# Two-kind attention and a max-out layer: casts by single heads, half copies, identity matmuls in TensorE's early gaps, and SyncE's closing block at another place in the code

## The chip, the cores and the metric

One core of one Trainium2 chip. The metric is the time of one execution on the device, in microseconds (us). A core has five engines with queues of their own: TensorE (PE; its weight loads are shown as PEld), VectorE (DVE), ScalarE (ACT), GpSimd (POOL) and SyncE (SP), which here issues every DMA.

## The reference

Attention over 4 batches of 8 heads, 768 tokens, 64 numbers a head, and on its output a layer that takes the larger of two products:

```
scores = q @ k.T / sqrt(64)
keep   = causal                                  for "retrieval" heads (3 of the 8: 0, 2, 6)
keep   = causal & (key < 4 | query - key < 64)   for the others
a      = softmax(where(keep, scores, -1e9))
x      = concat over heads of (a @ v)            [3072, 512]
out    = maximum(x @ w1, x @ w2) @ w_out         w1, w2: [512, 1024], w_out: [1024, 512]
```

All inputs and the output are float32. `is_retrieval` is data, so which heads are of which kind is known only when the program runs.

## The kernel before

**Two programs in one.** The kernel sorts the heads at run time. If exactly three are retrieval heads, a branch (`tc.If`, L830) takes the program `run(..., exact=True)`; otherwise it takes a general one. Each engine has both in its code, one behind the other, and behind them a closing block (the rows of L870) that all engines run at the end. With these inputs the first branch is taken, so at its end every engine jumps over the second.

**The order is planned.** `run` doesn't issue instructions. It records operations in a plan: a function that emits them, a cost for each engine that could do it, what it depends on, its buffers and a priority. `Plan.schedule` then plays time forward with these costs, gives each operation to the engine that can start it first, and the operations are emitted in the order of their planned starts. So a cost that is changed changes which engine does what, and in which order, all through the kernel. Each engine runs its own list strictly in that order.

**Attention.** Work goes by pairs of heads, four pairs a batch, 16 in all (`pair`). For a pair SyncE loads q, k and v, one DMA for each head (L671); into nine `ld` buffers, so three pairs' loads can be under way. Each DMA waits for the one eight before it. In batch 0 the first half of all of v comes ahead of everything (L320). Casts to bf16 (L300 on DVE and POOL, L298 on ACT) make `qb` and `vb`; six transposes each on TensorE (L692) turn q and k, and a copy of 768 columns brings them from PSUM to `qk` (`tok` sets the tokens in order). Scores (L578) come in tiles of two banks, the mask is added by matmuls with the identity in batch 0 (L586) or multiplied in later; ACT takes the exponential (L599); TensorE multiplies by v (L623) into one of two `po` banks, and DVE normalises (L639, L642) into `xs`. In the exact program one `po` bank is given over to the general PSUM pool after the second half-unit (`PO_TWO`, L640 to L646).

**The layer.** max(x w1, x w2) w_out is rewritten as relu(x (w1 - w2)) w_out + x (w2 w_out). So the weights are prepared once: casts of w2 and w_out (`w_bf`, `wo_bf`), the difference `wd_bf` (L443), transposes of w2 (L452, copied into the tile `raw`) and the product of w2 and w_out (L463, into `wm_bf`). They are loaded in quarters of 512 KB, on the same SyncE queue as q, k and v; `EARLY` names the one that is issued first, and `LATER` gives the others a priority in units of pairs. For each batch `x_turn` transposes x, and `dense` does the products (L756, L780, L787), the relu (L764, L766) and the store (L793).

**The start.** A block of 42 identity matmuls (L418) is the first operation on TensorE, planned at `WARM` = 4.6 us:

```
def warm(e, bk=bk):
    for _ in range(int(WARM / 0.107)):
        nc.tensor.matmul(bk.t[:, 0, 0:128], lhsT=ident, rhs=ident, start=True, stop=True)
```

Of the kernel before, what the change touches and what calls it, by code (L numbers as in the profile page):

```python
# [10 lines left out]
BF16 = mybir.dt.bfloat16  # L11
I32 = mybir.dt.int32
ALU = mybir.AluOpType
ACT = mybir.ActivationFunctionType
# [156 lines left out]
DMA_FIRST = -2.2  # L171
# [1 line left out]
WIDE_PAIRS = (1, 1, 1, 1, 1, 1, 1, 1, 1, 0, 0, 0, 0, 0, 0, 0)  # L173
X_XBAR = (0, 1, 1, 1)
EARLY = (('wo', 3),)
LATER = {('w2', 0): 3.93, ('w2', 1): 3.55, ('w2', 2): 3.4, ('w2', 3): 3.03, ('w1', 0): 5.86, ('w1', 1): 4.21, ('w1', 2): 6.83, ('w1', 3): 6.11, ('wo', 0): 3.53, ('wo', 1): 1.32, ('wo', 2): 0.84, ('wo', 3): 0.93}
MASK_TO = 1
NORM = 0.80
PO_TWO = 2
DUO_FROM = 1  # L180
WARM = 4.6

SHIFT = {}
HOLD = {}
# [3 lines left out]
def kernel(  # L188
# [19 lines left out]
    nc = tc.nc  # L208
    V = nc.vector
    B, H, S, D = q.shape  # L210
# [28 lines left out]
    ident = tl("ident", [128, 128])  # L239
# [51 lines left out]
    po_t = psum("po", 2)  # L291
# [4 lines left out]
    def copy(e, o, i):  # L296
        if e == "ACT":
            nc.scalar.copy(out=o, in_=i)  # L298
        else:
            issued[e].append((V if e == "DVE" else nc.gpsimd).tensor_copy(out=o, in_=i).ins)  # L300
# [75 lines left out]
    def run(full, head, col, exact):  # L376
        P = Plan(*((SHIFT, HOLD) if exact else ({}, {})))
# [4 lines left out]
        sc_p, po_p, mm_p = map(Pool, map(list, (sc_t, po_t, mm_t) if PO_TWO or not exact else (sc_t, po_t[:1], po_t[1:] + mm_t)))  # L382
# [27 lines left out]
                            in1=causal, op0=ALU.mult, op1=ALU.add)  # L410
            c_m = P.op(f, {"DVE": 5.0}, [d_ir], prio=-20)

        if exact:
            bk = Buf(mm_p)

            def warm(e, bk=bk):
                for _ in range(int(WARM / 0.107)):
                    nc.tensor.matmul(bk.t[:, 0, 0:128], lhsT=ident, rhs=ident, start=True, stop=True)  # L418
            P.op(warm, {"PE": WARM}, (), [bk], prio=-100)
        d_w = {}  # L420
        for name in ("w2", "w1", "wo"):
            for c in range(4):
                if (name, c) in EARLY:
                    P.number += 1
                else:
                    d_w[name, c] = P.op(lambda e, name=name, c=c: load_weight(name, c), {"SP": 0.5},
                                        prio=LATER[name, c], size=0.524, rate=0.35)

        def landed(*keys):

            return dict(deps=[d_w[k] for k in keys if k in d_w],
                        ready=max([0.0] + [DMA_FIRST + 6.05 + 1.7 * EARLY.index(k) for k in keys if k in EARLY]))
        wd_ops, w2_ops, wo_ops, wm_ops, w2t_ops = [], [], [], [], []
        for c in range(4):
            w2_ops.append(P.op(lambda e, c=c: copy(e, w2_bf[(slice(None),) + quarter(c)], w_raw[1][(slice(None),) + quarter(c)]),
# [10 lines left out]
        for fch in range(FC):  # L446
            bk = Buf(mm_p)
# [6 lines left out]
            o = P.op(tr, {"PE": 0.23}, w2_ops[2 * (fch // 4):2 * (fch // 4) + 2], [bk], prio=300 + fch)  # L454
# [15 lines left out]
        last_exp, last_score, last, last_open, units = [None], [None], [None], [None], [0]  # L470
# [50 lines left out]
        def attend(b, p, qk, vb, tk, ov, r):  # L521
# [110 lines left out]
            for u in range(2):  # L632
                rz = Buf(rz_p)

                def norm(e, u=u, rz=rz):
                    nh = 2 if exact else 1
                    p4 = po[u].t[:, 0, 0:nh * nn * (D + 1)].rearrange("p (h n e) -> p h n e", h=nh, e=D + 1)
                    rz_ = rz.t.rearrange("p (h n) -> p h n", h=nh)
                    V.reciprocal(out=rz_, in_=p4[:, :, :, D])  # L639
                    for i in range(nh):  # L640
                        h, n0 = (i, u * nn) if exact else (u, 0)
                        V.tensor_tensor(out=xs[b].t[:, n0:n0 + nn, bass.ds(col(s0 + h), D)], in0=p4[:, i, :, 0:D],  # L642
                                        in1=rz_[:, i].unsqueeze(2).to_broadcast([128, nn, D]), op=ALU.mult)
                done.append(P.op(norm, {"DVE": NORM}, [o for o in prev[u] if o], [po[u], rz, xs[b]], prio=r))
                for g in [u] if exact else range(NG):
                    norms[b][g].append(done[-1])  # L646
                units[0] += 1
                if exact and units[0] == PO_TWO:
                    spare = Buf(po_p)
                    spare.users = 1  # L650
                    P.op(lambda e: None, {"SP": 0.0}, [done[-1]], [spare], prio=-50).then = lambda: (
                        mm_p.free.append((spare.free, len(mm_p.tiles))), mm_p.tiles.append(spare.t))
            return done[-1]

        def tok(t):
            return t.rearrange("c (p n) -> c p n", n=NB)

        def pair(b, p):
            r = b * HP + p
            s0 = 2 * p  # L660
            if p == 0:
                xs[b], xt[b], xt_ops[b], norms[b] = Buf(xs_p), Buf(xt_p), [], ([], [])
            raws, loads = [], []
            for i, src in enumerate((q, k, v)):
                t = Buf(ld)
                raws.append(t)
                order, rate = ("(p n)", WIDE) if wide[r] and src is not v else ("(n p)", NARROW)
                two = []
                n0 = NB // 2 if b == 0 and src is v else 0
                for h in range(2):  # L670
                    two.append(P.op(lambda e, t=t, src=src, h=h, order=order, n0=n0: nc.sync.dma_start(  # L671
                        out=t.t[:, h, n0:], in_=src[b, bass.ds(head(s0 + h), 1), 128 * n0:].rearrange(
                            f"o {order} d -> p (o n) d", p=128)),
                        {"SP": 0.5}, (), [t], prio=r + 0.01 * i, size=0.0983 if n0 else 0.197, rate=rate))
                loads.append(two)
            qk, vb = Buf(qk_p), Buf(vb_p)
            tk, cast = [], []
            qb = Buf(qb_p)
            for i in range(2):
                def f(e, i=i):  # L680
                    for h in range(2):
                        copy(e, qb.t[:, i, :, h, :], raws[i].t[:, h])
                cast.append(P.op(f, {"POOL": 0.95, "DVE": 0.75} if b == 0 else {"POOL": 0.95}, loads[i],
                                 [raws[i], qb], prio=r + 0.01 * i, shared=True))
                if not wide[r]:
                    continue
                bk = Buf(mm_p)

                def tr(e, i=i, bk=bk):
                    psb = bk.t[:, 0].bitcast(BF16)  # L690
                    for n in range(NB):
                        nc.tensor.transpose(psb[:, n * 128:(n + 1) * 128],  # L692
                                            qb.t[:, i, n].rearrange("p h d -> p (h d)"), ident)
                o = P.op(tr, {"PE": 0.34}, [cast[i]], [qb, bk, qk], prio=90 + 2 * r)
                tk.append(P.op(lambda e, bk=bk, i=i: copy(
                    e, tok(qk.t[:, i]), bk.t[:, 0].bitcast(BF16)[:, 0:S].rearrange("c (n p) -> c p n", p=128)),
                               {"DVE": 0.90, "ACT": 0.7}, [o], [bk, qk], prio=r))
            if not wide[r]:
                tk.append(P.op(lambda e: nc.sync.dma_start_transpose(
                    out=qk.t.rearrange("c i (n p) -> c (i n) p", p=128),  # L700
                    in_=qb.t.rearrange("p i n h d -> p (i n h d)")),
                    {"SP": XBAR}, cast, [qb, qk], prio=r - 0.5, size=0.393, rate=0.2))
            n0 = NB // 2 if b == 0 else 0
# [13 lines left out]

            last[0] = attend(b, p, qk, vb, tk, ov, r)
# [91 lines left out]
                pool.free = []  # L810
        last[0].then = widen
        order = P.schedule()
        held = None
        with tc.manual_schedule():
            for o in order:
                for l in issued.values():
                    l.clear()
                o.emit(o.engine)
                if o.engine == "DVE" and o.shared:
                    held = issued["DVE"][-1]  # L820
                elif o.engine == "POOL" and held is not None:
                    tc.add_manual_dep(issued["POOL"][0], held.name, IN_TURN, reason="turns at the shared port")
                    held = None
# [51 lines left out]
```

## Time and profile before

| | |
|---|---|
| time, median of 6 runs | 189.69 us (189.13 to 191.44) |
| the profiled execution | 189.74 us, of which the span is 187.97 us |
| granted TensorE clock, mean over the span | 0.977 |
| busy: PE, PEld | 170.2 us (91%), 100.7 us (54%) |
| busy: ACT, DVE, POOL | 115.1 us (61%), 88.0 us (47%), 49.6 us (26%) |
| DMA | 36.96 MB, mean 197 GB/s |
| code: queue 8 (TensorE's) and 14 | 15 packets, 0.25 MB; 17 packets, 0.14 MB |

The page divides the span into 40 slices of 4.7 us. A digit is the busy share of a slice in tenths, and PEclk is the clock that was granted to TensorE, in tenths of full speed; where the trace records none, it stands at full. "SPq" and "PEldq" are rows of an engine's sequencer: waits, branches and DMA issues, in which the engine itself does nothing. A wait is put down to what came last before it ended. The chain that ended last is followed back from the last piece of work, and so says nothing of what comes behind it: the time from the last eviction to the end of the span is seen in the sequencers' rows alone.

### The profile page before, as it was taken

The numbers are of one execution on the slowest core, as the hardware profiler recorded it, in microseconds if no ns is written. First come the engines' busy times: TensorE is split into PE (matmuls) and PEld (weight loads), VectorE is DVE, ScalarE is ACT, GpSimd is POOL, SyncE is SP. The second block draws the span as 40 slices with busy tenths as digits, with TensorE's granted clock in tenths as the row PEclk, the third lists the DMA queues.
The fourth block names the chain that finished last, engine by engine and source line by source line (L and its number), as shares of the span: only waits on it lengthen the run. The fifth ranks groups of instructions, "written<-read, shape, count | busy, mean of one in ns | idle before, by whom it ended". The sixth has DMA issues, their size and how long they took to land.

```text
span 188.0 us, 4584 instructions
## 1 busy us (share of the span) xinstructions
PE 170.2 (91%) x1643; PEld 100.7 (54%) x1663; DVE 88.0 (47%) x247; ACT 115.1 (61%) x191; POOL 49.6 (26%) x107
## 2 busy tenths in 40 slices
PE   1859989699999999999999999999999999999950
PEld 1836756456756555654655555455545546445440
DVE  5647874868788385435575464446731000000000
ACT  3247898778888778727893395478836327337120
POOL 2101040556985864532026326010000000000000
PEclk9975999999999999999999999999999999999997
DMA  5999999999999999999999999991029221021040
GB/s 122 304 275 357 276 278 377 277 301 302 320 275 237 201 224 220 248 195 221 249 233 229 249 208 248 260 252 63 3 81 202 58 112 56 0 112 59 17 158 9
DMA packets 79554, 36.96 MB, mean 197 GB/s; under 512 B 68642, under 2 KB 73506, under 8 KB 79522
## 3 DMA queue, kind: packets, MB, share of 16 engines
q1 hardware_dynamic: 79522, 36.58, 77.2%
q8 instruction: 15, 0.25, 0.5%
q14 instruction: 17, 0.14, 0.2%
HBM read 25.17 MB, written 6.29 MB: 167 GB/s over the span
## 4 chain that ended last, share of the span: by engine, by line
PE 82%; DMA 4%; DVE 3%; ACT 2%; issue 2%; DVEq 0%; SPq 0%; POOL 0%; POOLq 0%
PE mm L756 12%; PE mm L780 11%; PE sc L578 9%; PE po L623 8%; PE po L756 8%; PE po L780 7%; PE mm L787 6%; PE sc L780 4%; PE po L787 3%; PE mm L463 3%; DMA raw<-in_moe_w_dram 3%; PE sc L756 2%; PE sc L787 2%; PE mm L692 2%; DMA ld<-in_k_dram 2%
## 5 line engine op out<-in xcount | busy, mean ns | idle before, releaser
L599 ACT ACTIVATE at_all<-sc 128x1024 bf16<-128x1024 f32 (+2 forms) x72 | 59.5, 870 | 6.6 <-PE sc L578 3.3
L756 PEld LDWEIGHTS <-wd_bf 128*128 128x128 bf16 x256 | 23.2, 98 | 14.0
L300 POOL CAST qb<-ld 128x384 bf16<-128x384 f32 x50 | 24.0, 507 | 18.9 <-DVE at_all L610 8.7
L756 PE MATMUL mm<-xt,wd_bf 128*128 128x384 bf16 x140 | 27.6, 326 | 0.0
L623 PE MATMUL po<-vb,at_all 128*128 128x65 bf16 x472 | 26.3, 195 | 0.8 <-POOL vb L300 0.7
L623 PEld LDWEIGHTS <-at_all 128*128 128x128 bf16 x472 | 21.6, 98 | 9.9 <-issue 2.1
L578 PE MATMUL sc<-qk 64*128 64x128 bf16 (+2 forms) x364 | 23.3, 242 | 1.9 <-ACT qk L298 0.9
L642 DVE TENSOR_TENSOR xs<-po,rz 128x192 f32 x64 | 22.9, 357 | 3.0 <-DVE rz L639 0.9
L780 PEld LDWEIGHTS <-raw 128*128 128x128 bf16 x152 | 14.1, 98 | 13.6
L578 PEld LDWEIGHTS <-qk 64*128 64x128 bf16 x364 | 12.7, 95 | 14.6 <-issue 9.4
L300 POOL CAST vb<-ld 128x384 bf16<-128x384 f32 (+1 forms) x28 | 12.9, 485 | 23.1 <-DVE qb L300 9.5
L639 DVE RECIPROCAL rz<-po 128x6 f32<-128x6 f32 x32 | 6.2, 194 | 26.4 <-PE po L623 26.3
L756 PE MATMUL po<-xt,wd_bf 128*128 128x384 bf16 x88 | 17.9, 326 | 0.0
L780 PE MATMUL mm<-wo_bf,raw 128*128 128x512 bf16 x59 | 15.5, 379 | 0.3
L610 DVE TENSOR_TENSOR at_all<-at_all,smk 128x1024 bf16<-128x1024 bf16 (+3 forms) x27 | 15.2, 583 | 0.0
L787 PEld LDWEIGHTS <-xt 128*128 128x128 bf16 x100 | 9.3, 97 | 9.3
L610 DVE TENSOR_TENSOR at_all<-at_all,tri 128x256 bf16<-128x256 bf16 (+1 forms) x36 | 9.7, 302 | 6.5 <-ACT at_all L599 6.4
L787 PE MATMUL mm<-wm_bf,xt 128*128 128x512 bf16 x48 | 12.3, 379 | 0.0
L298 ACT COPY ot<-mm 128x512 f32<-128x512 f32 x9 | 5.3, 586 | 11.1 <-PE mm L787 10.6
L764 ACT ACTIVATE raw<-mm 128x384 bf16<-128x384 f32 x20 | 9.8, 491 | 2.9 <-PE mm L756 2.6
L780 PE MATMUL po<-wo_bf,raw 128*128 128x512 bf16 (+1 forms) x45 | 10.8, 360 | 0.2
L298 ACT COPY qk<-mm 128x768 bf16<-128x768 bf16 x9 | 7.2, 805 | 4.6 <-PE mm L692 4.0
(91 smaller groups left out, 188.2 us busy)
## 6 DMA issues: line engine op xcount, KB each, us to landing
ld<-in_q_dram SPq DMA_DIRECT2D x32, 192.0 KB, 4.8
ld<-in_k_dram SPq DMA_DIRECT2D x32, 192.0 KB, 4.6
out_dram<-ot SPq DMA_DIRECT2D x23, 256.0 KB, 2.5
ld<-in_v_dram SPq DMA_DIRECT2D x24, 192.0 KB, 4.1
raw<-in_moe_w_dram SPq DMA_DIRECT2D x8, 512.0 KB, 6.5
raw<-in_moe_w_out_dram SPq DMA_DIRECT2D x4, 512.0 KB, 5.3
xt<-in_v_dram SPq DMA_DIRECT2D x3, 256.0 KB, 3.9
ld<-in_v_dram SPq DMA_DIRECT2D x8, 96.0 KB, 4.0
```

The lines of the kernel that those rows point to most:

```text
L298: nc.scalar.copy(out=o, in_=i)
L300: issued[e].append((V if e == "DVE" else nc.gpsimd).tensor_copy(out=o, in_=i).ins)
L578: nc.tensor.matmul(sc.t[:, k, off:off + w], lhsT=qk.t[64 * h:64 * h + 64, 1, j * 128:(j + 1) * 128], rhs=qk.t[64 * h:64 * h + 64, 0, q0:q0 ...
L599: nc.scalar.activation(out=a.t[:, k:k + m, 0:n], in_=sc.t[:, k:k + m, 0:n], func=ACT.Exp, scale=scale, bias=0.0 if bias is None else bias[ ...
L610: issued["DVE"].append(V.tensor_mul(out=y, in0=y, in1=z).ins)
L623: nc.tensor.matmul(po[u].t[:, 0, o:o + D + 1], lhsT=a.t[:, k, off + t * 128:off + (t + 1) * 128], rhs=vb.t[:, h, j, :], **fresh(u))
L639: V.reciprocal(out=rz_, in_=p4[:, :, :, D])
L642: V.tensor_tensor(out=xs[b].t[:, n0:n0 + nn, bass.ds(col(s0 + h), D)], in0=p4[:, i, :, 0:D], in1=rz_[:, i].unsqueeze(2).to_broadcast([128, ...
L756: nc.tensor.matmul(bk.t[:, 0, 0:GT], lhsT=wd_bf[:, c, f * 128:(f + 1) * 128], rhs=xt[b].t[:, g * NB // NG:(g + 1) * NB // NG, c, :], start ...
L764: nc.scalar.activation(out=gt.t[:, f, :], in_=bk.t[:, 0, 0:GT], func=ACT.Relu)
L780: nc.tensor.matmul(bk.t[:, 0, 0:m1 - m0], lhsT=gt.t[:, f, t * 128:(t + 1) * 128], rhs=wo_bf[:, f, m0:m1], start=(f == 0), stop=False)
L787: nc.tensor.matmul(bk.t[:, 0, 0:m1 - m0], lhsT=xt[b].t[:, c0 // 128, c, :], rhs=wm_bf[:, c, m0:m1], start=False, stop=(c == KC - 1))
```

## The change

- **Casts by single heads.** In batch 0 the cast of q or k for a pair was one operation of two instructions, planned when both heads had landed. It is now two operations, each depending on its own load.
- **Copies in halves.** In batch 0 the copy of the turned q or k to `qk` is two operations of 384 columns (tokens 0 to 383, 384 to 767), each for whichever engine is free first.
- **Gaps filled.** The block of 42 identity matmuls is gone. When the operations are emitted, each gap of over 0.2 us that the plan has on TensorE, as long as the work before it ends before 45 us of the plan's time, is filled with identity matmuls of 112 columns into the last columns of a `po` bank: 58 ahead of the first transposes, then 8, 19, 12, 7, 4, 6, 3, 6, 2 and 3.
- **Closing block moved.** SyncE gets 60 drains at the end of the branch that isn't taken.
- **Planned costs.** The issue of a load is planned at 0.55 us instead of 0.5, the first weight half a microsecond later, and all of `LATER` is new. On SyncE this moves one quarter of w2 from behind the fourth pair's loads to ahead of the second pair's, and the last two quarters of w1 stay behind the seventh pair's; the number of loads is the same. In the early stage several casts and copies change engines.

```diff
-LATER = {('w2', 0): 3.93, ('w2', 1): 3.55, ('w2', 2): 3.4, ('w2', 3): 3.03, ('w1', 0): 5.86, ('w1', 1): 4.21, ('w1', 2): 6.83, ('w1', 3): 6.11, ('wo', 0): 3.53, ('wo', 1): 1.32, ('wo', 2): 0.84, ('wo', 3): 0.93}
+LATER = {('w2', 0): 3.982944845571182, ('w2', 1): 3.713032602722715, ('w2', 2): 3.1258011363789584, ('w2', 3): 0.06184797336222103, ('w1', 0): 4.719495772014594, ('w1', 1): 5.936357867710815, ('w1', 2): 6.682884501259243, ('w1', 3): 7.846850994116073, ('wo', 0): 1.8083697110576127, ('wo', 1): 3.159407628162693, ('wo', 2): 0.46232370355043345, ('wo', 3): 1.9016815755209604}
...
-WARM = 4.6
+WARM = 45.0
+PAD = 60
...
-        if exact:
-            bk = Buf(mm_p)
-
-            def warm(e, bk=bk):
-                for _ in range(int(WARM / 0.107)):
-                    nc.tensor.matmul(bk.t[:, 0, 0:128], lhsT=ident, rhs=ident, start=True, stop=True)
-            P.op(warm, {"PE": WARM}, (), [bk], prio=-100)
...
-                        ready=max([0.0] + [DMA_FIRST + 6.05 + 1.7 * EARLY.index(k) for k in keys if k in EARLY]))
+                        ready=max([0.0] + [DMA_FIRST + 6.55 + 1.7 * EARLY.index(k) for k in keys if k in EARLY]))
...
+                    given.append(spare)
...
-                        {"SP": 0.5}, (), [t], prio=r + 0.01 * i, size=0.0983 if n0 else 0.197, rate=rate))
+                        {"SP": 0.55}, (), [t], prio=r + 0.01 * i, size=0.0983 if n0 else 0.197, rate=rate))
...
-                def f(e, i=i):
-                    for h in range(2):
-                        copy(e, qb.t[:, i, :, h, :], raws[i].t[:, h])
-                cast.append(P.op(f, {"POOL": 0.95, "DVE": 0.75} if b == 0 else {"POOL": 0.95}, loads[i],
-                                 [raws[i], qb], prio=r + 0.01 * i, shared=True))
+                one_ = []
+                for hs in ((0,), (1,)) if b == 0 else ((0, 1),):
+                    def f(e, i=i, hs=hs):
+                        for h in hs:
+                            copy(e, qb.t[:, i, :, h, :], raws[i].t[:, h])
+                    one_.append(P.op(f, {"POOL": 0.48, "DVE": 0.38} if b == 0 else {"POOL": 0.95},
+                                     [loads[i][h] for h in hs], [raws[i], qb], prio=r + 0.01 * i, shared=True))
+                cast += one_
...
-                o = P.op(tr, {"PE": 0.34}, [cast[i]], [qb, bk, qk], prio=90 + 2 * r)
-                tk.append(P.op(lambda e, bk=bk, i=i: copy(
-                    e, tok(qk.t[:, i]), bk.t[:, 0].bitcast(BF16)[:, 0:S].rearrange("c (n p) -> c p n", p=128)),
-                               {"DVE": 0.90, "ACT": 0.7}, [o], [bk, qk], prio=r))
+                o = P.op(tr, {"PE": 0.34}, one_, [qb, bk, qk], prio=90 + 2 * r)
+                for p0, p1 in ((0, 64), (64, 128)) if b == 0 else ((0, 128),):
+                    w = (p1 - p0) / 128
+                    tk.append(P.op(lambda e, bk=bk, i=i, p0=p0, p1=p1: copy(
+                        e, tok(qk.t[:, i])[:, p0:p1],
+                        bk.t[:, 0].bitcast(BF16)[:, 0:S].rearrange("c (n p) -> c p n", p=128)[:, p0:p1]),
+                                   {"DVE": 0.1 + 0.8 * w, "ACT": 0.1 + 0.65 * w}, [o], [bk, qk], prio=r))
...
+        spin = po_t[1 - given[0].slot if given else 0]
...
+                if exact and o.engine == "PE":
+
+                    gap = o.start - idle - (0.1 if idle else 0.5)
+                    if gap > 0.1 and idle < WARM:
+                        for _ in range(int(gap / (0.055 if idle else 0.093))):
+                            nc.tensor.matmul(spin[:, 0, 400:512], lhsT=ident, rhs=ident[:, 0:112], start=not idle,
+                                             stop=True, skip_group_check=True)
+                    idle = o.end
...
+        with tc.manual_schedule():
+            for _ in range(PAD):
+                nc.sync.drain()
```

More of the change, by code (lines that the diff above doesn't have):

```diff
@@ L469, in run @@
         xs, xt, xt_ops, norms = {}, {}, {}, {}
-        last_exp, last_score, last, last_open, units = [None], [None], [None], [None], [0]
+        last_exp, last_score, last, last_open, units, given = [None], [None], [None], [None], [0], []
         def exp_op(emit, n, pointer, deps, bufs, prio):
@@ L812, in run @@
         order = P.schedule()
-        held = None
+        held, idle = None, 0.0
+        spin = po_t[1 - given[0].slot if given else 0]
         with tc.manual_schedule():
             for o in order:
+                if exact and o.engine == "PE":
[5 more added lines that the diff above has]
+                    idle = o.end
                 for l in issued.values():
```

## The prediction

> **What bounds the kernel now.** I read the page's slices first, then busy time by stretch, then the chain that ended last, then the queues' own instructions after TensorE's last matmul. All sums are made against the profiled execution: 189.74 us, of which 187.97 are the span and 1.77 lie around it; the median of the six runs is 189.69, so the two can be taken as one.
>
> ```profile
> PE   1859989699999999999999999999999999999950
> PEclk9975999999999999999999999999999999999997
> DMA  5999999999999999999999999991029221021040
> ```
>
> TensorE is full from the eighth slice to the last but two: from about 36 us its work alone sets the pace, and nothing in the change touches that work. So the time is the moment at which TensorE becomes full, plus a constant, plus the tail. The second row shows half clock near the start. By stretch (columns: us, then busy time of PE, PEld, DVE, ACT, POOL, granted clock, DMA share, GB/s):
>
> ```profile
> 8.53:11.95 3.42, 1.22 (x15) 0.71 (x13) 2.12 (x6) 1.10 (x2) 0.00 (x0) 0.99 0.87 262
> 11.95:15.36 3.41, 2.83 (x23) 1.39 (x24) 1.68 (x4) 2.11 (x3) 0.00 (x0) 0.50 1.02 319
> 15.36:18.77 3.41, 3.41 (x34) 2.40 (x33) 2.27 (x4) 2.43 (x3) 0.64 (x2) 0.51 1.07 359
> ...
> 22.00:24.00 2.00, 2.00 (x33) 1.55 (x34) 1.93 (x8) 1.98 (x5) 0.84 (x3) 1.00 0.78 196
> 24.00:26.00 2.00, 1.69 (x23) 1.06 (x21) 1.78 (x5) 2.00 (x4) 1.45 (x5) 1.00 0.84 201
> ...
> 34.00:36.00 2.00, 1.07 (x14) 0.82 (x14) 1.92 (x7) 1.19 (x2) 1.11 (x3) 1.00 0.98 201
> ```
>
> TensorE works 1.22 of 3.42 us up to 11.95 and the clock falls to 0.5; it returns at 18.77, after a stretch without a gap. Half clock on 2.83 + 3.41 us of work costs 3.1 us of TensorE time. But TensorE then idles 3.0 us between 20 and 36 (its eight two-us stretches sum to 12.97 of 16). What it waits for at the end of that time is in the chain (start us, us, what):
>
> ```profile
> 22.43 5.00 DMA raw<-in_moe_w_dram
> 27.46 0.70 DVE w_bf L300
> ...
> 34.37 0.70 DVE w_bf L300
> 35.12 0.40 PE mm L452 x4
> ...
> 37.15 0.86 PE mm L463 x4
> ```
>
> The last quarter of w2 is issued at 24.59, lands 9.8 us later (34.34), and its cast starts at 34.37, its transposes (L452) at 35.12, the product of w2 and w_out (L463) at 36.99. From there TensorE never stops. The transfers land one behind another all the way: q and k halves 0.53 us apart, 512 KB weights 1.4 to 2.0.
>
> **The tail.** TensorE ends at 181.2, the last eviction at 181.6, the span at 188.0. SyncE's own rows:
>
> ```profile
> L830 SPq COMPARE_BRANCH  x1: 46/46/46, 182.0 to 182.0; - x1
> ```
> ```profile
> L870 SPq EVENT_SEMAPHORE  x4: 17/28/28, 184.6 to 184.8; - x4
> ```
> ```profile
> L870 SPq EVENT_SEMAPHORE  x6: 17/28/28, 186.9 to 187.9; - x6
> ```
> ```profile
> q14 instruction: 1, 0.01, 3.2%
> ```
>
> SyncE jumps at 182.0 over the branch not taken, runs four instructions of the closing block from 184.6 to 184.82, stands still, and goes on at 186.85. Nothing that it waits for ends then: the fifth waits for a store that was issued well before the last one, and the last store (1.9 us to landing) is in by 183.6. The last row is the transfers of 185.2 to 185.8: one 8 KB packet of instructions. So the closing block crosses a boundary of the code between its fourth and fifth instruction, and the crossing costs 186.85 - 184.82 = 2.03 us, less the 0.07 between neighbours: 1.96.
>
> **The change, part by part.**
>
> *Closing block moved.* 60 drains in the branch not taken, which never run. The built programs differ on SyncE by 1 instruction fewer in the branch taken and 57 more in the other (60 drains, 3 waits fewer), so the closing block moves by 56. Its size of a code block: TensorE runs 3306 instructions (x1643 and x1663) and fetches 12 packets of 16 KB before its closing jump, some 256 instructions each, so 8 KB are about 128. The boundary was 4 behind the block's start; it is now 52 ahead of it, and 13 instructions fit whether a block is 128 or 256. Minus 2.0. The first fetch after the jump (2.5 us) stays. The other engines reach the end at 182.4 (PE) and 183.9 (ACT), before SyncE at 184.6, and hide as before. The Trainium skill ("Runtime: NRT & Kernel Launch", section "Instruction fetch mechanics") says that crossing a code boundary is mostly hidden behind the slower issue; by that this part would be worth nothing and the sum would be 189.1. The rows above disagree: an engine that has just jumped has nothing to hide it behind.
>
> *Matmuls in the gaps.* 42 identity matmuls go (4.55 us, 108 ns each), 58 come ahead of the first transposes and 70 into ten later gaps (8, 19, 12, 7, 4, 6, 3, 6, 2, 3). The 58 take 112/128 of 108 ns, 95 each: 5.5 us, to 9.7 us at the latest, before the first transposes are due at 9.96. The later ones, at the 55 ns that four transposes in 0.22 us show, take 3.9 us. I expect the clock to stay at 1.00, since at 32 to 36 us TensorE worked 2.5 of 4 us and kept it. The pure price of the clock is then up to 3.1 us; how much of it reaches the end is decided below. The last five stand behind 36 us: 0.3 us if no gap is there.
>
> *Single casts.* No cost and no gain: in the trace each of the two casts of a pair already starts on its own landing (9.00 and 9.54). What changes is who does them: seven early q, k casts on POOL instead of two, 0.48 each, next to a POOL that is idle for 9 us there.
>
> *Copies in halves.* A whole copy takes 0.80 on ACT, 0.96 on DVE; a half isn't shown. Bounds: half (0.40, 0.48) and the whole; I take 0.45 and 0.5. The second half waits for the first, on the other engine. For the first pair the ACT half of k ends at 12.10 instead of 12.45 and the first scores, which need that half alone, start 0.4 earlier. The DVE half stands behind a v cast that waits for its landing at 12.26, so it ends at 13.15; the second tile of scores waits for it, behind the first exponential anyway. With full clock the six exponentials run without a break from 12.9 and end near 18.6 instead of 20.17.
>
> *Order of the weights.* One w2 quarter moves from behind the fourth pair's loads to ahead of the second pair's, past 18 loads on SyncE. It adds its 0.5 us of issue and 1.4 to 2.0 us to every landing of pairs two to four. The second pair's last cast, at 16.44 before, ends at 17.9; its copies to qk stand on DVE behind the first pair's reciprocal, a register load (0.62) and two normalisations (0.75), so its scores start near 20, as before (19.95). The first pair's gain is given back there.
>
> *Where the gain goes.* In front of the last w2 quarter stand the same bytes as before, and no transfer there waits for TensorE. It should land at 34.34 again and the w2 product start at 37.0, however fast TensorE was before. That is the core of this forecast: most of the 3.1 us becomes idle time before 35. Bounds on the landing: between 22 and 26 us the transfers ran at 198 GB/s, against 378 from 26 to 34; if that lull goes, 4 x (378 - 198)/378 = 1.9 us earlier. On the other side, 172 more TensorE instructions bring code fetches forward, so that a third falls before the landing; behind the fetch at 19.26 a k load landed 1.98 after its neighbour instead of 0.53: 1.4 later. The first fetch now falls near 14 us, where two 512 KB weights are queued and a lull is less likely, so I lean to the gain: minus 0.6.
>
> Sum: 189.74 - 2.0 - 0.6 = 187.1.
>
> The Trainium skill ("TensorE: Matmul & The Clock Gate", Part 1) says of the warm-up that its penalty is under 1% of a typical span. By it the fill would bring less than 1.9 us, and the sum would lie above 185.8.
>
> **The rivals.**
> - *The lull goes too* (22%). For it: the halves keep DVE and ACT ahead of the casts, ACT was busy 15.2 of the 18 us from 18 to 36. Against: the transfers wait for each other, not for casts. 189.74 - 2.0 - 1.9 = 185.8.
> - *An extra code fetch holds back the last w2 quarter* (14%). For it: the late k load above. 189.74 - 2.0 + 1.4 = 189.1.
> - *The closing block still crosses a boundary* (7%): the shift isn't 56, or another engine now stalls. 189.74 - 0.6 = 189.1.
> - *Slower* (7%): the second pair. Its loads come up to 2.0 later, and its copies on DVE stand behind 1.4 us of the first pair's end. It decides if the second pair's first scores start later than 23 us, that is, by more than the 3.0 us of idle time that TensorE has before 36 to absorb it, and ACT, then the last, passes the whole on: 189.74 - 2.0 + 3.4 = 191.1.
>
> **How the numbers follow.** The forecast (50%) is 187.1, from 186.3 to 188.0 by itself. The range, 185.4 to 188.9, takes in the first rival and most of the doubt on the landing and leaves out the other three but for their edges. A measurement of this kernel can tell about 1% (1.9 us) from no change: faster by that is below 187.8, which is 0.42 of the forecast's 0.50 and all of the first rival; slower by that, above 191.6, is the tail of the last one.
>
> **What would show it.** Right: SyncE's closing block runs through without the 2 us stop; PEclk stays at full from 8.5 us on; first exponential near 12.9; second pair's scores near 20; the last w2 cast again near 34.4 and L457 near 37; more idle (or identity matmuls) on TensorE before it. Wrong, if the w2 product starts two microseconds earlier (the clock did reach the end), or later than 38; if the stop at the end is still there; or if TensorE has gaps between 37 and 180.

## The result and the profile after

The changed kernel takes 190.88 us (median), the kernel before 189.74 in the same comparison: ratio 1.0053, 95% interval 1.0036 to 1.0070. It is slower by half a per cent, a small loss whose interval leaves out 1, where 187.1 was forecast. All ratios here are of executions within 1.5% of their kernel's fastest. The profiled execution took 191.08 us, its span 188.90.

The tail came out as forecast. SyncE's rows after its branch:

```profile
L841 SPq COMPARE_BRANCH  x1: 46/46/46, 184.8 to 184.8; - x1
L885 SPq EVENT_SEMAPHORE  x10: 17/28/28, 187.6 to 188.8; - x10
```

The ten instructions that stood in two groups, 2 us apart, now run in one. From TensorE's last matmul to the end of the span it is 4.93 us instead of 6.79: 1.86 less. But TensorE's last matmul ends at 183.98 instead of 181.18. So 2.8 us were lost ahead of the tail. The page's slices:

```profile
PE   1984999599999999999999999999999999999990
PEclk9999699999999999999999999999999999999997
DMA  5989979999999999999999999994015713012022
```

From the ninth slice on TensorE is as full as before; the loss lies ahead of 40 us. By stretch (us, then busy PE, PEld, DVE, ACT, POOL, granted clock, DMA share, GB/s):

```profile
16.00:18.00 2.00, 0.19 (x7) 0.07 (x3) 1.20 (x2) 1.18 (x2) 0.00 (x0) 1.00 0.95 287
18.00:20.00 2.00, 1.09 (x17) 0.79 (x18) 1.45 (x6) 0.55 (x2) 0.28 (x1) 0.93 0.92 284
20.00:22.00 2.00, 2.00 (x27) 1.63 (x25) 1.87 (x5) 1.24 (x2) 0.81 (x3) 0.50 1.07 372
...
36.00:38.00 2.00, 0.44 (x9) 0.44 (x9) 1.44 (x4) 1.24 (x2) 0.50 (x1) 1.00 1.18 276
```

There are two holes, at 16 to 19 and at 36 to 38 us, and the clock falls behind the first. What TensorE waited for from 8 to 40 us (us in total, times, longest):

```profile
PE mm L690 <- DVE qb L301: 3.4, 3, 2.7
PE po L824 <- DVE xs L636: 1.8, 1, 1.8
```

The first hole in the chain that ended last (start us, us, what):

```profile
10.60 7.87 DMA ld<-in_q_dram
...
18.49 0.37 DVE qb L301
...
18.91 0.51 PE mm L690 x6
19.41 0.33 PE sc L572 x4
19.74 0.64 PE po L617 x10
...
21.88 0.65 PE po L824 x7
22.53 0.56 PE po L617 x10
...
23.11 0.21 DVE rz L633
...
23.34 0.37 DVE xs L636
...
23.82 0.39 PE sc L572 x5
```

The second pair's q lands at 17.93 and 18.46 us (before: 14.40 and 14.94), behind the w2 quarter, which itself took from 12.13 to 16.12 to land. TensorE's list has that pair's transposes (L690) ahead of the first pair's last scores (L572 at 19.41), so the first pair stands still too. The second pair's own first scores start 3.1 us later than before (start us, us, engine, line; before, then after):

```profile
19.95 0.40 PE L578 MATMUL sc<-qk 64*128 64x384 bf16 x6
```
```profile
23.01 0.44 PE L572 MATMUL sc<-qk 64*128 64x384 bf16 x6
```

The early quarter also holds up what is issued behind it, since each DMA waits for the landing of the one eight before it. SyncE's longest wait between 8 and 22 us is for that quarter:

```profile
SPq L310 <- DMA raw<-in_moe_w_dram: 1.5, 1, 1.5
```

It issues the w_out quarter that comes next at 16.14, as the w2 quarter lands (16.12), the third pair's q at 17.48 instead of 13.90, and the first weight behind the fourth pair at 25.93 instead of 22.43.

The second hole:

```profile
27.49 8.42 DMA raw<-in_moe_w_dram
...
35.93 0.07 DVE w_bf L301
36.00 0.54 issue
36.54 0.20 DVE rz L633
...
36.76 0.37 DVE xs L636
...
37.15 0.37 DVE xs L636
...
37.56 0.46 PE po L824 x6
38.02 0.22 PE po L446 x4
...
39.92 0.86 PE mm L457 x4
```

w2's last quarter lands at 35.91 instead of 34.34 and its cast is done at 36.62. The transposes of it (L446) start at 38.02: ahead of them stand six identity matmuls (L824), which write into a `po` bank and so wait until VectorE has normalised what is in it (L636). The product of w2 and w_out (L457) starts at 39.92 instead of 37.15 (the chain of before shows it at 37.15; its own start, 36.99, lies a little earlier, since a row of the chain begins where the row before it ends): here are the 2.8 us by which TensorE ends later.

### The profile page after: what moved, and what is told of

Read it like the earlier page. It is cut to its first block, busy times and chain, and to the rows that moved or that the text cites. A ratio compares the mean times of both kernels' runs of the same rounds, so it can differ in the third digit from the quotient of the medians.

```text
span 188.9 us, 4765 instructions
## 1 busy us (share of the span) xinstructions
PE 172.9 (92%) x1728; PEld 104.9 (56%) x1749; DVE 88.6 (47%) x252; ACT 113.6 (60%) x189; POOL 51.4 (27%) x112
## 4 chain that ended last, share of the span: by engine, by line
PE 80%; DMA 9%; SPq 2%; issue 1%; DVE 1%; ACT 0%
PE mm L781 12%; PE mm L757 12%; PE po L617 8%; PE sc L572 8%; PE po L757 8%; PE mm L788 6%; PE po L781 5%; DMA raw<-in_moe_w_dram 4%; DMA ld<-in_q_dram 4%; PE sc L781 4%; PE po L788 3%; PE sc L757 2%; PE mm L690 2%; PE sc L788 2%; PE po L457 2%; PE mm L457 2%
## 5 line engine op out<-in xcount | busy, mean ns | idle before, releaser
L301 POOL CAST qb<-ld 128x384 bf16<-128x384 f32 x55 | 26.2, 506 | 37.9 <-DVE at_all L604 17.3
L617 PE MATMUL po<-vb,at_all 128*128 128x65 bf16 x472 | 27.0, 197 | 0.2 <-DVE xs L636 0.2
L757 PE MATMUL mm<-xt,wd_bf 128*128 128x384 bf16 x140 | 26.7, 326 | 0.0
L636 DVE TENSOR_TENSOR xs<-po,rz 128x192 f32 x64 | 22.9, 357 | 2.5 <-DVE rz L633 0.3
L572 PE MATMUL sc<-qk 64*128 64x128 bf16 (+2 forms) x364 | 22.4, 235 | 0.1
L572 PEld LDWEIGHTS <-qk 64*128 64x128 bf16 x364 | 12.4, 94 | 12.4 <-issue 9.3
L781 PE MATMUL mm<-wo_bf,raw 128*128 128x512 bf16 (+1 forms) x74 | 18.4, 367 | 0.4 <-issue 0.2
L301 POOL CAST vb<-ld 128x384 bf16<-128x384 f32 (+1 forms) x28 | 12.9, 486 | 13.6 <-PE po L617 4.3
L824 PE MATMUL po<-ident 128*128 128x112 bf16 x128 | 10.9, 256 | 6.0 <-DVE pcol L347 4.2
L604 DVE TENSOR_TENSOR at_all<-at_all,smk 128x1024 bf16<-128x1024 bf16 (+3 forms) x27 | 15.1, 579 | 0.0
L788 PE MATMUL mm<-wm_bf,xt 128*128 128x512 bf16 (+1 forms) x55 | 13.9, 371 | 0.1
L824 PEld LDWEIGHTS <-ident 128*128 128x128 bf16 x128 | 9.6, 124 | 6.4 <-DVE pcol L347 4.2
L299 ACT COPY ot<-mm 128x512 f32<-128x512 f32 (+1 forms) x11 | 6.2, 567 | 11.1 <-PE mm L788 10.7
L604 DVE TENSOR_TENSOR at_all<-at_all,tri 128x256 bf16<-128x256 bf16 (+1 forms) x36 | 9.3, 292 | 6.7 <-ACT at_all L593 6.6
L301 DVE COPY qk<-mm 128x384 bf16<-128x384 bf16 (+1 forms) x14 | 9.1, 667 | 3.5 <-PE mm L690 2.6
```

What stands on the lines that cost most here:

```text
L572: nc.tensor.matmul(sc.t[:, k, off:off + w], lhsT=qk.t[64 * h:64 * h + 64, 1, j * 128:(j + 1) * 128], rhs=qk.t[64 * h:64 * h + 64, 0, q0:q0 ...
L604: issued["DVE"].append(V.tensor_mul(out=y, in0=y, in1=z).ins)
L617: nc.tensor.matmul(po[u].t[:, 0, o:o + D + 1], lhsT=a.t[:, k, off + t * 128:off + (t + 1) * 128], rhs=vb.t[:, h, j, :], **fresh(u))
L757: nc.tensor.matmul(bk.t[:, 0, 0:GT], lhsT=wd_bf[:, c, f * 128:(f + 1) * 128], rhs=xt[b].t[:, g * NB // NG:(g + 1) * NB // NG, c, :], start ...
L781: nc.tensor.matmul(bk.t[:, 0, 0:m1 - m0], lhsT=gt.t[:, f, t * 128:(t + 1) * 128], rhs=wo_bf[:, f, m0:m1], start=(f == 0), stop=False)
L788: nc.tensor.matmul(bk.t[:, 0, 0:m1 - m0], lhsT=xt[b].t[:, c0 // 128, c, :], rhs=wm_bf[:, c, m0:m1], start=False, stop=(c == KC - 1))
```

## The experiments

Every ratio is to the kernel before, run on the same chip beside it, with its 95% interval.

### The drains alone

The kernel before and this:

```diff
     with branch.Else():
         run([True] * H, lambda s: s, lambda s: s * D, False)
+        with tc.manual_schedule():
+            for _ in range(60):
+                nc.sync.drain()
```

> The kernel before with the 60 drains behind the Else branch and nothing else of the change. All theories of the early loss agree here: SyncE's last stop (2.0 us between two of its closing instructions in the profile of before) is gone, nothing early moves, and the end comes 1.9 to 2.0 us sooner: about 187.8 us against 189.74. If the stop was covered by something else, 189.7.

Measured: 187.95 us, ratio 0.9898 (0.9840 to 0.9957); from the last matmul to the end 4.80 us. Its closing block:

```profile
L875 SPq EVENT_SEMAPHORE  x10: 17/28/28, 185.2 to 186.5; - x10
```

So this part is worth what was forecast, and it is all that the change gains. The sentence of the Trainium skill that the prediction cited ("Runtime: NRT & Kernel Launch", "Instruction fetch mechanics"), that a crossing is mostly hidden, doesn't hold for this crossing, four instructions behind a jump: it cost 1% of the time.

### Matmuls and order of the weights, each taken back

```diff
 # e2, and e4: the 42 planned identity matmuls back, nothing in the gaps
+  ...
-                if exact and o.engine == "PE":
-                    gap = ...
 # e3, and e4: LATER as before
-LATER = {('w2', 0): 3.98..., ..., ('w2', 3): 0.06..., ...}
+LATER = {('w2', 0): 3.93, ..., ('w2', 3): 3.03, ...}
```

> The changed kernel with TensorE's early gaps left empty (the 42 identity matmuls of the kernel before are put back at the start); order of the weights, single-head casts, half copies and drains stay as changed. Theory A (the w2 quarter moved ahead of pair 1's loads makes the early loss of about 2.8 us): little changes, 190.3 us or more. Theory B (the identity matmuls make it, by standing ahead of real work in TensorE's queue and by fetching more code): about 188.1 us, with w2's product starting near 37.5 us. Theory C (the single-head casts and half copies load VectorE): no change, 190.9 us.

> The changed kernel with the due times of the weights as before, so that no w2 quarter is loaded between pair 0 and pair 1; identity matmuls, casts, copies and drains stay as changed. Theory A (order of the weights): pair 1's loads land some 3 us earlier, w2's last quarter near 34.3 us, about 188.2 us. Theory B (identity matmuls): 190.3 us or more. Theory C (casts and copies): no change, 190.9 us.

> Both taken back: no identity matmuls in the gaps and the weights' due times as before; single-head casts, half copies and drains are left of the change. Theories A and B, or both together: about 187.8 us, as with the drains alone. Theory C: the early loss stays, 190.9 us; a smaller loss of the casts and copies would show as the difference from the kernel before with drains alone.

| | w2 quarter ahead (changed) | as before |
|---|---|---|
| identity matmuls in the gaps | the changed kernel 1.0053 (1.0036 to 1.0070) | e3 0.9989 (0.9954 to 1.0024) |
| none | e2 0.9995 (0.9958 to 1.0032) | e4 0.9927 (0.9895 to 0.9960) |

Theories A and B are each half right: down either column the matmuls cost 0.6%, along either row the order costs 0.6 to 0.7%, and together they are the 1.3% between e4 and the changed kernel. In the traces the order of all other work is the same on every engine down a column (only PSUM banks change turns), so there the matmuls alone are compared, with their start (58 ahead of all work, or 42). Theory C falls: without both the early loss is gone, though casts and copies stay. Whether these and the planned costs cost anything, 0.9927 against 0.9898, the intervals don't tell.

How the order costs without any gap matmuls is seen by stretch in e2 and then in e4:

```profile
16.00:18.00 2.00, 1.25 (x14) 0.73 (x11) 1.39 (x4) 1.54 (x2) 0.00 (x0) 0.50 1.09 316
18.00:20.00 2.00, 2.00 (x24) 1.40 (x23) 1.58 (x5) 1.21 (x2) 1.09 (x3) 0.50 1.02 295
20.00:22.00 2.00, 2.00 (x29) 1.60 (x29) 1.46 (x3) 1.14 (x4) 0.00 (x0) 0.50 1.05 317
```
```profile
16.00:18.00 2.00, 2.00 (x21) 1.50 (x20) 1.35 (x4) 0.47 (x1) 0.65 (x2) 0.50 1.11 384
18.00:20.00 2.00, 2.00 (x36) 1.38 (x33) 1.22 (x3) 1.59 (x3) 0.51 (x1) 0.71 1.00 286
20.00:22.00 2.00, 1.85 (x36) 1.43 (x34) 1.55 (x6) 2.00 (x3) 0.00 (x0) 1.00 0.77 234
```

In e2 the second pair's q lands at 16.88 and 17.40 us (e4: 14.63 and 15.15). TensorE has a hole at 16 to 18 and then works at half clock until 24 instead of 19. A load goes out only when the DMA eight before it has landed: the third pair's q is issued at 16.37, as a w_out quarter lands (16.36; in e4 14.10 and 14.09), and what stands behind it keeps the lag. SyncE reaches the first weight behind the fourth pair at 24.09 instead of 22.33; w2's last quarter lands at 34.70 instead of 34.03, although it has one quarter less just ahead of it. TensorE ends 1.2 us later.

### The order alone

```diff
-LATER = {('w2', 0): 3.93, ..., ('w2', 3): 3.03, ...}
+LATER = {('w2', 0): 3.98..., ..., ('w2', 3): 0.06..., ...}
```

> The kernel before with the due times of the weights of the changed kernel, and nothing else of the change: a w2 quarter is loaded between pair 0 and pair 1. Theory A (the order costs by itself, since all behind it lands later): pair 1's loads land 1.5 to 3 us later and w2's last quarter near 35 us, some 1.2 us slower, 190.9 us. Rival (the order only costs together with the identity matmuls): 189.7 us.

Measured: 194.17 us, ratio 1.0227 (1.0180 to 1.0274): neither. Half of the 6.9 us by which TensorE ends later is there at w2's product, which starts 3.5 us later. Of that, theory A has the loads (second pair's q at 17.34 us, last w2 quarter at 35.29 instead of 34.34); besides, the transposes of w2 and what stands among them ran at a granted clock of 0.50, from 36.9 to 40.3 us. The rest comes later; the largest hole is in the chain at 77 us:

```profile
75.37 1.56 DMA ld<-in_q_dram
76.93 5.58 DMA qk<-qb
82.51 0.05 issue
82.55 0.61 PE sc L578 x10
```

There TensorE waits for a transpose by DMA; between 60 and 100 us it idles 2.9 us, in the kernel before 0.4. New due times are new decisions all through the plan, so this run can't price the early move alone; the pair e2 and e4 can.

### Where the matmuls cost

First the six ahead of w2's transposes, the only ones left out:

```diff
-                    if gap > 0.1 and idle < WARM:
+                    if gap > 0.1 and idle < WARM and not 27.9 < idle < 28.1:
```

> The changed kernel less the six identity matmuls that stand directly ahead of w2's transposes in TensorE's queue; every other instruction is the same. In the profile of the changed kernel they waited for VectorE's normalising and ran at 37.56 us, while the last cast that the transposes need had ended at 36.6. Theory Q (the identity matmuls cost by a wait that stands ahead of real work): the transposes start near 36.7 us, w2's product near 38.6 instead of 39.92, about 189.6 us. Theory F (they cost by fetching TensorE's code earlier and oftener, which holds up the loads): twelve instructions fewer change nothing, 190.9 us.

Measured: 190.56 us, ratio 1.0034 (1.0003 to 1.0065); 0.2% better than with them, inside the intervals, where 0.7% was expected. The product started at 37.91, 2 us sooner than in the changed kernel's profile, but TensorE ended only 0.4 us sooner. Most of the rest went at 50 us, where TensorE waits in this run and not in the changed kernel (waits from 40 to 60 us):

```profile
PE mm L690 <- POOL qb L301: 1.6, 1, 1.6
```

That cast of a later pair's q began at 50.62 on GpSimd (POOL), when VectorE's mask product (L604) ended; until 50.20 GpSimd had worked on a weight difference, begun as a quarter of w1 landed (47.78; in the kernel before that quarter landed at 45.30). So a second limit, of the later loads, stands behind w2's product, and an earlier product is not passed on whole. The drains alone show it too: the product's own start is 35.99 us, 1.0 sooner than in the kernel before, yet TensorE ends 0.6 later, and waits 0.7 us at 55.5 for a weight difference.

With the old order, by groups from the front (the first 58; 97; 122, which the expectation for it miscounts as 116; and the 122 with 16 columns):

```diff
-WARM = 45.0
+WARM = 25.0                   # e6 and e11: 122 matmuls; 10.0 in e10: 97; 1.0 in e9: 58
 # e11 also
-  nc.tensor.matmul(spin[:, 0, 400:512], lhsT=ident, rhs=ident[:, 0:112], ...)
+  nc.tensor.matmul(spin[:, 0, 400:416], lhsT=ident, rhs=ident[:, 0:16], ...)
```

> The weights' due times as before, and of the identity matmuls only those that the planner puts into gaps in the first 25 us (116 of them, none ahead of w2's transposes); casts, copies and drains as changed. Theory Q: as without any identity matmuls, about 188.3 us. Theory F: as with all of them in the old order, about 189.9 us. If filling the early gaps is worth something by itself: below 188.0 us.

> The weights' due times as before, and of the identity matmuls only the 58 that stand ahead of all real work on TensorE (in the run with all the early ones, 122 of them, the ratio was 0.9992, without any 0.9927). Theory T (the identity matmuls cost because those between real instructions hold these up: in that run pair 0's second and third exponential began 1.2 to 1.3 us later than without them): these 58 end before q's first transposes can start, so as without any, ratio about 0.993. Theory F (each instruction brings TensorE's code fetches forward, and these hold up the loads): about half of the loss, ratio about 0.996.

> The same with the first 97: 58 ahead of all work, 8 between the transposes of q and k, 19 between these and the first scores, 12 behind pair 0's second scores. Theory T: these 39 more are those that delay pair 0's exponentials, so nearly the whole loss is here, ratio 0.997 to 0.999. Theory F: in proportion to the instructions, 0.998. If the loss comes later (the 25 up to 25 us): 0.993.

> All 122 early identity matmuls at their places, but of 16 columns instead of 112: the same number of instructions and as much code, less time each. Theory T: they hold up less, most of the loss goes, ratio 0.993 to 0.995. Theory F: the code is the same, ratio 0.999 as with 112 columns.

Measured: 0.9972 (0.9936 to 1.0009) with 58, 1.0014 (0.9982 to 1.0047) with 97, 0.9992 (0.9958 to 1.0025) with 122, 0.9981 (0.9943 to 1.0020) with 122 short ones; none: 0.9927. The loss is there with the 97 already, so Q as one place is not enough, and shorter matmuls don't take it away, which T had expected (the interval just reaches T's 0.995). This left code (F) or what else changes at the start (the 58 are outside the plan and in another bank). Four runs on that:

```diff
 # e13: e4, and e14: the drains alone, with matmuls in the gaps behind the planned 42
+                    gap = o.start - idle - 0.1
+                    if gap > 0.1 and 0 < idle < 45.0:
+                        for _ in range(int(gap / 0.055)):
+                            nc.tensor.matmul(spin[:, 0, 400:512], lhsT=ident, rhs=ident[:, 0:112], ...)
 # the drains alone, the 42 at the start: e8 140 of 16 columns, e16 11 of 512, e15 42 of 112 ahead of the plan into po
 # e8
-                for _ in range(int(WARM / 0.107)):
+                for _ in range(140):
+                    nc.tensor.matmul(bk.t[:, 0, 0:16], lhsT=ident, rhs=ident[:, 0:16], start=True, stop=True)
 # e16
-                for _ in range(int(WARM / 0.107)):
+                for _ in range(11):
 # e15, without the planned block
+                for _ in range(42):
+                    nc.tensor.matmul(po_t[0][:, 0, 400:512], lhsT=ident, rhs=ident[:, 0:112], ...)
```

> The run without identity matmuls in the gaps (weights as before, single-head casts, half copies, drains; ratio 0.9927) with 106 identity matmuls of 112 columns put into TensorE's planned gaps, and nothing else: the 42 of the kernel before stay at the start, and each tile stays in its bank. Theory G (those in the gaps cost): ratio 0.998 to 1.000. Theory S (what costs is the start: 58 instead of the 42 ahead of all work, in another bank, with the banks behind them taken in another turn): 0.993.

> The same question on the other plan: the kernel before with the drains (ratio 0.9898) and 110 identity matmuls of 112 columns in the planned gaps, the 42 at the start kept. Theory G: ratio 0.995 to 0.997. Theory S: 0.990. If filling the gaps helps where the loads come early: below 0.988.

> The kernel before with the drains, the 42 identity matmuls written ahead of the plan into the attention's bank instead of being a planned operation in a bank of the pool; the order of all other work is the same, only their banks change turns. Theory S: ratio about 0.994. Theory G: 0.990, as with the drains alone.

> The kernel before with the drains, its 42 identity matmuls of 128 columns at the start made 140 of 16 columns: 196 instructions more on TensorE, all ahead of its first real work, nothing else changed. Theory F: TensorE's code is fetched at about 15, 25 and 36 us instead of 18, 30 and 39 us, the third fetch meets the loads of w2, and the time is 0.5 to 1.1 us above that of the drains alone, 188.5 to 189.0 us. Theory Q: the fetches come earlier but cost nothing, about 187.9 us. If the 140 take longer than the 4.5 us of the 42 and hold up the first transposes, it is slower early, before 13 us, and tells nothing.

> The kernel before with the drains, its 42 identity matmuls of 128 columns made 11 of 512 columns: the same time on TensorE at the start, 62 instructions less, so that its code is fetched some 2 us later each time. Theory F (code fetches ahead of w2's last landing are what identity matmuls cost): as good as the drains alone or better, ratio 0.985 to 0.990, w2's last quarter at or ahead of 33.3 us. If the place of the fetches doesn't matter: 0.990.

Measured: e13 1.0004 (0.9961 to 1.0047), e14 1.0006 (0.9973 to 1.0039): the matmuls in the gaps cost 0.8% and 1.1%, with start, banks and order left as they were. So G holds (in e14 the loss is larger than its 0.995 to 0.997), and S isn't needed for the loss; e15 by itself, 0.9931 (0.9896 to 0.9965), lies between what the two expected and doesn't decide. Code is not it as far as these show: 196 instructions more (e8) gave 0.9921 (0.9892 to 0.9950), 62 less (e16) 0.9966 (0.9932 to 1.0000), no better than the drains alone, if anything slower. But in e8 TensorE's code fetches began at 7.4, 21.3 and 33.5 us, not at 15, 25 and 36 as was expected. In the profiles of all kernels with matmuls in the gaps the first began between 14.3 and 15.8 us and the second between 21.7 and 25.2; no run has such a pair without them, so a cost of fetches at these places is not excluded.

The matmuls did keep the clock up: in e13's profile it never falls ahead of 184 us, in e4's it is at 0.50 from 12.3 to 19.1. What they cost is plainest in e13 against e4, since w2's last quarter lands at 34.10 and 34.03 us. A wait of TensorE from 8 to 40 us, e13 and then e4:

```profile
PE po L831 <- DVE xs L643: 2.1, 2, 1.3
```
```profile
PE mm L453 <- DVE w_bf L301: 0.4, 1, 0.4
```

And the chain at w2's transposes (L453), e13 and then e4:

```profile
34.39 0.33 DVE w_bf L301
34.72 0.18 issue
34.90 0.20 DVE rz L640
...
35.12 0.37 DVE xs L643
...
35.52 0.37 DVE xs L643
...
35.93 0.75 PE po L831 x12
36.68 0.22 PE mm L453 x4
```
```profile
34.49 0.61 DVE w_bf L301
35.10 0.05 issue
35.15 0.40 PE mm L453 x4
```

The twelve identity matmuls (L831) wait for VectorE and the transposes stand behind them: 36.68 instead of 35.15; w2's product starts 1.33 us later (38.58 against 37.25) and TensorE ends 1.47 later. In e14 the identity matmuls waited so three times, 3.0 us in all. Last, e13 without its last 19:

```diff
-                    if gap > 0.1 and 0 < idle < 45.0:
+                    if gap > 0.1 and 0 < idle < 25.0:
```

> The run with 106 identity matmuls in the gaps and banks and start as they were (ratio 1.0004) less the last 19: the 12 ahead of w2's transposes and three small groups behind them; 87 stay, the rest is the same. In that run's profile w2's last quarter landed at 34.10 us, as without any (34.03), but the 12 waited for VectorE's normalising and the transposes behind them began at 36.68 instead of 35.15. Theory Q (this one place is the cost): transposes near 35.2 us, w2's product near 37.3, ratio 0.993 to 0.995. If the ones in the gaps before 30 us cost by themselves: 0.998 to 1.000.

Measured: 189.53 us, ratio 0.9965 (0.9935 to 0.9994): half of the loss is back. In its profile the transposes follow the cast at once (36.17 to 36.22), but the first weight behind the fourth pair is issued at 24.34 instead of 22.33 and w2's last quarter lands at 35.42. On SyncE the lag begins at the third pair's q, issued at 15.38 as a w_out quarter lands (e4: 14.10), and grows where one issue at 22.90, just behind a code fetch at 22.81, takes 1.40 us. Neither is seen to wait for TensorE. And this profile, at 190.77 us, is the second slowest of its twelve executions, so it shows where time can go and not what the median lost. Both halves rest on intervals that overlap; how the early groups cost, and which of them, is open.

### Is the early clock worth anything

```diff
-                for _ in range(int(WARM / 0.107)):
+                for _ in range(1):
```

> The other end: the kernel before with the drains, and of its 42 identity matmuls at the start only one. The clock then stays low until the attention itself raises it; if the time is set by the loads up to 37 us, this costs nothing, ratio 0.989 to 0.993. If the warm-up reaches the end: the 3.4 us of full clock from 8.5 to 11.95 us, in which TensorE worked 1.2 us, are lost, 1.2 us more, ratio 0.996.

Measured: 188.80 us, ratio 0.9897 (0.9857 to 0.9937), the same as with all 42. Its stretch from 10 us:

```profile
10.00:12.00 2.00, 1.64 (x12) 1.11 (x12) 1.08 (x3) 0.81 (x2) 0.00 (x0) 1.00 1.01 274
```

The twelve transposes take 1.64 us where they took 0.97 in the kernel before, so TensorE is slow there (the clock row has no record yet and stands at full); by six transposes in 0.84 us at 15.83 and in 0.50 us at 17.41 it is so until about 17 us. It costs nothing at the end.

That takes the early clock away. The other direction, full clock nearly all through, stands in e15: of its twelve executions seven had a mean granted clock of 0.991 or more and took 188.6 us on average, five had 0.976 to 0.982 and took 188.4. So in one and the same kernel the early clock is worth nothing that can be seen.

### A version meant to beat both

```diff
-LATER = {..., ('w2', 2): 3.4, ('w2', 3): 3.03, ...}
+LATER = {..., ('w2', 2): 2.7, ('w2', 3): 2.6, ...}
```

> A version meant to beat both: the kernel before with the drains, and two w2 quarters issued ahead of pair 3's loads instead of behind them, into the stretch from 22 to 26 us in which the transfers run at some 200 GB/s because SyncE waits for buffers. If the stretch takes them up, w2's last quarter lands 1.5 to 2.5 us sooner than with the drains alone (33.3 us) and the time is 186.0 to 187.0 us, ratio 0.981 to 0.986. If pair 3's loads, some 2.7 us later, stop the attention, or the wait for buffers only moves with them: 188 to 190 us, ratio 0.990 to 1.000.

Measured: 189.99 us, ratio 0.9987 (0.9948 to 1.0026). The lull went: 340 and 326 GB/s from 22 to 26 us. But w2's last quarter landed at 33.48, no sooner than with the drains alone (33.32), and TensorE worked only 0.80 us of the two from 30 to 32: the fourth pair's first load landed 3.2 us later (25.37 against 22.19). The best version that was run is the drains alone, with 42 identity matmuls or with one: 0.990.

## Why the prediction was wrong

- **The tail, minus 1.96: right.** 1.86 in the changed kernel, 1.0% by itself.
- **"It adds its 0.5 us of issue and 1.4 to 2.0 us to every landing", scores of the second pair near 20: the first step that failed.** For the second pair's q it was 2.1 us in e5, 2.2 in e2, 2.9 in e7 and 3.5 in the changed kernel; the pair's last cast ended at 20.22 instead of 17.9, and its scores started at 23.01. What was overlooked is the order on TensorE, where the late pair's transposes stand ahead of the first pair's last scores, and on SyncE, where each DMA waits for the landing of the one eight before it.
- **"In front of the last w2 quarter stand the same bytes as before ... It should land at 34.34 again": failed.** It landed at 35.91. The bytes are the same, but their issue came 2.9 us later (27.49 instead of 24.59), with the lag that the third pair's q got from the landing eight before it (17.48 instead of 13.90). Up to 26 us both kernels had moved 6.7 MB; then, with the issues late, the lull that the kernel before has from 22 to 26 us came from 26 to 30 instead, 151 and 238 GB/s against 389 and 388:

```profile
26.00:28.00 2.00, 2.00 (x32) 1.51 (x28) 1.30 (x4) 2.00 (x4) 1.43 (x4) 1.00 0.56 151
```

  So the lull of the first rival moved and did not go. The lean of 0.6 to the gain had the wrong sign.
- **The matmuls in the gaps, priced at 0.3 us at most: failed.** They were priced as work in empty time. They are instructions in a queue, with a wait of their own on the bank into which they write, and real work is behind them: 0.6 to 1.1%, in four pairs of kernels. The wait ahead of w2's transposes is shown; what the earlier groups cost by is open.
- **Clock at 1.00 from 8.5 us on: wrong** from 19.7 to 23.1 us, behind the first hole. **That a gain in clock does not reach the end: right**, by e18 and by the two kinds of execution of e15.
- **The halves:** 0.48 us on ACT and 0.55 on DVE, near the 0.45 and 0.5 that were taken. The first exponential started at 13.41 instead of 12.9; the sixth ended at 21.74 instead of 18.6, since the first pair's last scores stood behind the late transposes.
- **"So the time is the moment at which TensorE becomes full, plus a constant": right for the kernel before and the changed one** (144.2 us from the product's own start to TensorE's end in both), not in general: 145.8 in the drains alone and 145.9 in e5, which wait again near 50 and 55 us.
- **The rivals.** The one held at 7%, slower by the second pair, names the place (first scores later than 23 us; they started at 23.01, just at its edge) and its time, 191.1, is near the measured one by luck. But its price, ACT passing on the delay, is not what the traces show at w2's product: late loads and matmuls ahead of the transposes do. The extra code fetch did not come as such: the third fetch began at 35.81, as the quarter landed.

By ratios: drains with casts and copies 0.9927 (e4), order +0.7% (e2), gap matmuls +0.6%: 1.0053.

## What to carry to other kernels

An instruction that fills a gap of the plan is only free if it can start at once and nothing behind it becomes ready sooner than planned; look first into which tile it writes, and who must have read that tile. A transfer that is moved forward is to be priced on everything that waits for the loads behind it, and then on what stands behind those waits in an in-order queue. Ask before you raise the clock of an engine whether a run with the clock left low is any slower.

## What the runs showed of the hardware that was not expected

- In two runs a DMA issue of SyncE that began just behind one of TensorE's code fetches took 1.05 us (e13, at 15.34, fetch at 15.04) and 1.19 us (e6, at 23.42, fetch at 23.27), where its neighbours took 0.33 to 0.49. Nothing here isolates it, and a fetch is not the only thing that goes with a long issue: one at 11.13 in the changed kernel took 1.52 us, with the first fetch at 15.50.
- The same 512 KB quarter at the same place in the queue landed 4.0 us behind its forerunner in the changed kernel, 3.6 in e2, 1.75 in e5 and 2.1 in e7. Counted from its issue it is 7.2, 6.2, 5.8 and 6.2 us: where it landed close, the forerunner was late.
